# Spreading an expert search over the matrix work of a fused linear-attention and mixture-of-experts kernel

## The chip, the cores and the metric

The kernel runs on one core of a Trainium2 chip. The time is the device time of one execution in microseconds; three executions of the kernel before gave 408.66, 408.78 and 409.49, so the median is 408.78. A profile of one further execution shows where the time goes. Its engines are called PE (matrix products; PEld is the loading of their stationary operand), DVE (vector), ACT (scalar), POOL (GpSimd, which here also issues indirect DMAs) and SP (which issues the other DMAs).

## The reference

The first part is a linear-attention recurrence over 4 batches, 8 heads, 768 steps and a head size of 48. Its output, seen as 3072 rows (tokens) of 384 numbers, is the input of a mixture of 8 experts with a balanced assignment:

```python
logits = x @ w_gate                      # 3072 x 8
order = np.argsort(-logits.flatten())
for idx in order:                        # greedy, largest logit first
    tok, e = idx // E, idx % E
    if assigned[tok] >= 0 or counts[e] >= cap: continue     # cap = 384
    assigned[tok] = e; counts[e] += 1
for e in range(E):
    h = np.maximum(x[assigned == e] @ w1[e], 0.0)           # 384 -> 1024
    out[assigned == e] = h @ w2[e]                          # 1024 -> 384
```

Each expert gets exactly 384 tokens. The reference run on the given inputs fills the experts in the order 4, 3, 7, 5, 0, 6, 2, 1.

## The kernel before

**Two halves.** The class `Mild` computes the attention, in 24 units of 128 tokens, and writes the rows to memory. The class `Assignment` (called `walk`) finds the assignment without the sort: it repeatedly finds the next expert that fills up, with its 384 tokens. One such finding is called a search here. The class `Experts` multiplies: for each expert it gathers the 384 rows (`gather`, indirect DMAs on POOL), loads two weight matrices of 1.5 MB (`load_weights`, on SP), turns the rows (`turn`, L1509), computes the hidden layer (`hidden`, 24 products `h_ps`, L1518), and the second layer.

**A search** (`likely_steps`) is a generator that stops at each `yield`. It has three rounds. In a round DVE compares all tokens with 16 thresholds (`ind`), PE counts (`counts`, L925, three small products), DVE makes `own`, `cnt` and `wide`, PE adds over the partitions (`counts`, L936), and DVE narrows the thresholds (`most`, `full`, `dg`, `cand`, `low`). After the third round DVE makes `acc` and PE `st_ps` (L1056, L1057). `tokens` turns the found set into a list of row numbers: `row`, `oh`, `vals` on DVE, `some_ps` on PE (L1389), `part`, `list_ps` (L1407), `tok`. `book` checks what was found and `leave` takes its tokens out. Every round thus goes from DVE to PE and back twice.

**The early star.** Before all logits are known, one expert is chosen as the star (expert 1 with these inputs, the last to fill) and 256 of its tokens are computed early, by `early` of `Experts` (`e_xT_ps`, `e_h_ps`, `e_o_ps`), in pieces that `go(m)` interleaves with the searches for the first and second expert. Its last 128 tokens are computed at the end.

**Second layer.** Experts 1 to 5 in order of finding take two of their three token blocks by a scheme of seven products instead of eight (`seven`): sums of blocks of the hidden layer (S1 to S4, 128x512) and of the weights (T1 to T4, 128x768), made on DVE by `sums_of` (L1569), then seven groups of four products `p_ps` (L1591) and `SEVEN_OUT` sums (L1600). The third block is computed plainly by `result` (eight products `o_ps`, L1618). Experts 6 and 7 use a scheme of fifteen products. The tiles of the T sums have one buffer each, so expert n+1's T3 can be written only when PE has used expert n's.

**The order.** `run` loops over the experts. At its top it pulls the generator `later` until that yields a fetched expert; during the products it pulls twice more (`at_product`). Since the star can be among the experts found, `later` waits with a fetch: expert n is fetched only when the search after it is done, and `choose` takes the later one if the star has passed. `walk.ok` is cleared when a check fails, and at the end a branch on it (`If`) computes everything again in a general way. The attention, the early pieces and the first searches have an order written out by hand (`manual_schedule`); from `x.open_rest` on, a scheduler sets the order of each engine's instructions when the kernel is built.[...]

## Time and profile before

| what | value |
|---|---|
| median of three runs | 408.78 us |
| profiled execution | 408.76 us |
| its span in the profile | 406.9 us |
| PE busy | 383.4 us, 94% |
| DVE busy | 272.6 us, 67% |
| ACT, POOL busy | 160.6 us, 141.2 us |
| granted PE clock, mean | 0.992 |
| memory traffic | 139 GB/s over the span |

The span is from the first to the last event of the profile; 1.86 us of the execution lie outside it. The page cuts the span into 40 slices; the attention lies in the first thirteen or so, the experts after it. In the timeline view a line gives a start, a duration, engine, line of the program, operation and tiles, the number of records, and in brackets how long the engine had been idle and what ended it. A product of 32-bit numbers leaves two records.

### The profile page before, as it was taken

To read this page: it belongs to the slowest core of one execution; us is meant where nothing else is said; L and a number is where in the kernel's file an instruction comes from. 1 tells how busy PE (TensorE), PEld (TensorE's weight loads), DVE (VectorE), ACT (ScalarE), POOL (GpSimd) and SP (SyncE) were. 2 spreads that over 40 slices of the span, in tenths; PEclk is the share of its full clock that TensorE was granted. 3 is DMA by queue.
4 is the path that set the end of the run, shared out by engine and by line. 5 is a ranking of instruction groups with operands and counts; after the bars stand their busy time and mean duration, and the time that the engine had idled before them with its cause. 6 is when DMAs were issued, how large, how long until landed. Compare 5 with 4: busy or idle time off the path is not lost. (4 is left out here: it accounts for less than half of the span.)

```text
span 406.9 us, 8688 instructions
## 1 busy us (share of the span) xinstructions
PE 383.4 (94%) x3236; PEld 290.0 (71%) x3236; DVE 272.6 (67%) x948; ACT 160.6 (39%) x419; POOL 141.2 (35%) x173
## 2 busy tenths in 40 slices
PE   7789999999999887998999999999999999999993
PEld 5678888788877654568558657756856956966991
DVE  6675777576885788889387577578658852971630
ACT  4887878788872310221221221222212312132130
POOL 8787877666732021103303303202302222040020
PEclk9999999999999999999999999999999999999998
DMA  9999998887591282009218109108217365180010
GB/s 120 163 178 196 191 185 165 154 166 154 131 314 40 80 287 100 20 4 345 77 47 324 40 23 363 43 19 313 76 39 246 122 215 214 34 335 21 2 60 26
DMA packets 95331, 57.29 MB, mean 141 GB/s; under 512 B 77232, under 2 KB 89520, under 8 KB 95280
## 3 DMA queue, kind: packets, MB, share of 16 engines
q1 hardware_dynamic: 91520, 47.19, 46.4%
q0 software_dynamic: 3104, 9.44, 6.5%
q8 instruction: 27, 0.44, 0.5%
q14 instruction: 24, 0.20, 0.2%
q10 hardware_dynamic: 656, 0.01, 0.1%
HBM read 47.20 MB, written 9.44 MB: 139 GB/s over the span
## 5 line engine op out<-in xcount | busy, mean ns | idle before, releaser
L1518 PE MATMUL h_ps<-xT,w 128*128 128x384 f32 (+1 forms) x384 | 122.1, 469 | 0.6 <-ACT xT L1510 0.6
L1518 PEld LDWEIGHTS h_ps<-xT,w 128*128 128x128 f32 x384 | 65.6, 190 | 36.7 <-issue 3.6
L1520 ACT ACTIVATE hid<-h_ps 128x384 f32<-128x384 f32 (+1 forms) x64 | 29.7, 464 | 93.3 <-PE h_ps L1518 89.8
L1494 POOL DMA_INDIRECT xg<-x_rows,tok x22 | 22.9, 1039 | 112.3 <-issue 69.6
L494 ACT ACTIVATE AT<-ident,dd 128x128 f32<-128x128 f32 x192 | 58.8, 390 | 3.4 <-DVE dd L448 3.4
L1612 POOL DMA_INDIRECT out_dram<-o_all,to x16 | 19.9, 1247 | 75.8 <-DVE o_all L1600 73.7
L507 DVE COPY_PREDICATED AT<-mask,g_ps 128x512 f32<-128x512 uint8 x48 | 32.6, 733 | 12.5 <-PE g_ps L503 12.2
L1595 ACT COPY res<-p_ps 128x384 f32<-128x384 f32 (+2 forms) x28 | 13.2, 473 | 59.0 <-PE p_ps L1591 59.0
L1618 PE MATMUL o_ps<-w,hid 128*128 128x384 f32 x96 | 32.8, 486 | 0.0
L503 PE MATMUL g_ps<-rT,kT 48*128 48x128 f32 x384 | 28.6, 290 | 0.6 <-DVE AT L507 0.6
L436 POOL TENSOR_TENSOR kss<-krs,wk 128x384 f32<-128x384 f32 x24 | 24.3, 1014 | 9.3 <-DVE krs L340 8.1
L503 PEld LDWEIGHTS g_ps<-rT,kT 48*128 48x128 f32 x384 | 24.1, 193 | 3.8 <-PE rT_ps L458 1.1
L541 PE MATMUL y_ps<-AT,vts 128*64 128x128 f32 x384 | 25.7, 276 | 0.0
L443 POOL TENSOR_TENSOR rk<-rk,u_bc 128x384 f32<-128x384 f32 x24 | 24.2, 1007 | 1.9
L442 POOL TENSOR_TENSOR rk<-krs 128x384 f32<-128x384 f32 x24 | 24.5, 1021 | 0.2 <-DMA krs<-in_r_dram 0.2
L1618 PEld LDWEIGHTS o_ps<-w,hid 128*128 128x128 f32 x96 | 17.4, 190 | 9.8
L541 PEld LDWEIGHTS y_ps<-AT,vts 128*64 128x64 f32 x384 | 20.6, 137 | 1.0 <-issue 0.3
L1569 DVE TENSOR_TENSOR H<-hid 128x512 f32<-128x512 f32 x12 | 7.9, 687 | 19.1 <-ACT hid L1520 19.1
L1591 PE MATMUL p_ps<-T,S 128*128 128x192 f32 x120 | 20.7, 327 | 0.0
L559 ACT COPY x<-y_ps 128x512 f32<-128x512 f32 x24 | 14.0, 583 | 16.0 <-PE y_ps L541 16.0
L1591 PEld LDWEIGHTS p_ps<-T,S 128*128 128x128 f32 x120 | 19.6, 190 | 0.0
L477 DVE TENSOR_TENSOR rT<-rT_ps,WR 112x512 f32<-112x512 f32 x23 | 15.8, 685 | 4.4 <-PE rT_ps L458 4.4
(303 smaller groups left out, 687.4 us busy)
## 6 DMA issues: line engine op xcount, KB each, us to landing
w<-in_moe_w_dram SPq DMA_DIRECT2D x18, 1536.0 KB, 9.0
krs<-in_k_dram SPq DMA_DIRECT2D x24, 192.0 KB, 4.2
krs<-in_r_dram SPq DMA_DIRECT2D x24, 192.0 KB, 4.7
vts<-in_v_dram SPq DMA_DIRECT2D x24, 192.0 KB, 4.7
x_rows<-xr SPq DMA_DIRECT2D x24, 192.0 KB, 3.1
xg<-x_rows,tok POOLq DMA_INDIRECT x22, 4.4
out_dram<-o_all,to POOLq DMA_INDIRECT x16, 2.9
out_dram<-o_sb,to POOLq DMA_INDIRECT x5, 2.6
```

The source lines that it names most:

```text
L436: self.nc.gpsimd.tensor_mul(self.kss[:, n % self.NS].rearrange("p (g h) d -> p g h d", g=2)[:, :, :, 0:D], src, self.wk.rearrange("p (g h) ...
L442: nc.gpsimd.tensor_mul(rk, self.krs[:, n % self.NK, 1, 0:H, 0:D], self.krs[:, n % self.NK, 0, 0:H, 0:D])
L443: nc.gpsimd.tensor_mul(rk, rk, self.u_bc)
L494: nc.scalar.mul(AT[:, z, a, :], self.ident, dd[:, h:h + 1])
L503: nc.tensor.matmul(g_ps[:, z, a, :], kT[rows, a, :], rT[rows, a, :], start=True, stop=True)
L507: nc.vector.copy_predicated(out=AT[:, z], mask=self.mask.unsqueeze(1).to_broadcast([128, HP, T]), data=g_ps[:, z])
L541: nc.tensor.matmul(yv[q * PD:(q + 1) * PD, o // 2, o % 2, :], lhsT, rhs, start=(o // 2, q) not in seen, stop=stop, skip_group_check=True)
L1494: nc.gpsimd.indirect_dma_start(out=xg[:, c, :], out_offset=None, in_=x_dram[0:within, :], in_offset=bass.IndirectOffsetOnAxis(ap=tok[:, c: ...
L1518: nc.tensor.matmul(h_ps[:, 0:m], w1[:, f, ts(j, 128)], xT[:, f, 0:m], start=(f == 0), stop=(f == KD - 1))
L1520: nc.scalar.activation(hid[:, j, 0:m], h_ps[:, 0:m], AF.Relu)
L1591: nc.tensor.matmul(ps[:, q, :], left[a][:, j, :], right[b][:, j, :], start=(j == 0), stop=(j == KF // 2 - 1))
L1618: nc.tensor.matmul(o_ps, hid[:, j, ts(c, 128)], w2[:, j, :], start=(j == 0), stop=(j == KF - 1))
```

## The change

Experts two to four are fetched as soon as their own search is done, without the search that follows. For them `book(first=True)` is used, which clears `ok` if the found expert is the star: that case is left to the general part. From expert five on the former scheme holds. The search steps during experts 1, 2 and 3 are given out at 5, 7 and 9 points, counted in a progress from 0 to 2 (hidden layer 0 to 1, products 1 to 2), instead of two points in the products. The T sums of the first expert run come after its first sum of the hidden layer, and not before the hidden layer. The pieces of the star's second layer are grouped differently among the steps of the second search.

```diff
-        def hidden(self, w1, xT, m, half=lambda hid: None):
+        def hidden(self, w1, xT, m, half, progress):
...
                 if j == KF // 2 - 1:
                     half(hid)
+                progress((j + 1) / KF)
...
-                nc.vector.tensor_tensor(out=t, in0=at[a], in1=at[b], op=op)
+                last = nc.vector.tensor_tensor(out=t, in0=at[a], in1=at[b], op=op)
                 at[name] = t
+            return last
...
-        def run(self, ahead, later, rows):
-            xT = self.turn(ahead)
+        def run(self, ahead, later, rows, pulls={}):
+            xT, lead = self.turn(ahead), True
             while ahead:
...
-                right = (self.fifteen_w2 if many else self.seven_w2)(w2) if whole else None
+                late, lead = lead and not many, False
+                right = (self.fifteen_w2 if many else self.seven_w2)(w2) if whole and not late else None
                 left = {}
+                some = pulls.get(n, 2)
+                due = [1.55, 1.75] if some == 2 else [0.75 + 1.15 * i / (some - 1) for i in range(some)]
 
                 def half(hid):
+                    nonlocal right
                     for name, (i, j) in self.BLOCKS.items():
                         left[name] = hid[:, ts(j, KF // 2), ts(i, 128)]
-                    self.sums_of(left, self.EARLY_SUMS if many else self.SEVEN_EARLY)
+                    last = self.sums_of(left, self.EARLY_SUMS if many else self.SEVEN_EARLY)
+                    if late:
+                        with tc.issue_after(last.ins):
+                            right = self.seven_w2(w2)
+
+                def progress(t):
+                    nonlocal xT
+                    while due and t > due[0]:
+                        due.pop(0)
+                        next(later, None)
+                        if many and not due and ahead:
+                            xT = self.turn(ahead)
 
                 def at_product(part):
-                    nonlocal xT, stage
-                    if stage == 0 and part > 0.55 or stage == 1 and part > 0.75:
-                        next(later, None)
-                        stage += 1
-                        if many and stage == 2 and ahead:
-                            xT = self.turn(ahead)
+                    progress(1 + part)
...
-                go(6)
-                for m in (2, 3, 2, 3):
+                go(8)
+                for m in (2, 4, 2, 99):
                     next(search)
                     go(m)
-                go(99)
...
             walk.bound(ident)
-            was = second
+            now = second
+            for n in range(2, 5):
+                walk.book(now, first=True)
+                yield x.fetch(n, now["fmax"], walk.tokens(now["place"]))
+                walk.leave(now)
+                yield
+                now = walk.new_outs()
+                yield from walk.likely_steps(**now)
+            was = now
             walk.book(was)
             walk.leave(was)
-            for n in range(2, E):
+            for n in range(5, E):
...
-        x.run((1, xg, to, *have["v"]), later(), (a for a in [*out_rows[2:NT - 1], None]))
+        x.run((1, xg, to, *have["v"]), later(), (a for a in [*out_rows[2:NT - 1], None]),
+              {1: 5, 2: 7, 3: 9})
```

More of the change, by code (lines that the diff above doesn't have):

```diff
@@ L1522, in hidden @@
                     half(hid)
+                progress((j + 1) / KF)
             return hid
-        BLOCKS =        BLOCKS = dict(h0=(0, 0), h1=(0, 1), h2=(1, 0), h3=(1, 1), h4=(2, 0), h5=(2, 1))
+        BLOCKS = dict(h0=(0, 0), h1=(0, 1), h2=(1, 0), h3=(1, 1), h4=(2, 0), h5=(2, 1))
         SEVEN_EARLY = (("S3", "h0", SUB, "h2"),)
@@ L1634, in run @@
                 ahead = next((a for a in later if a), None)
-                right = (self.fifteen_w2 if many else self.seven_w2)(w2) if whole else None
+                late, lead = lead and not many, False
+                right = (self.fifteen_w2 if many else self.seven_w2)(w2) if whole and not late else None
                 left = {}
+                some = pulls.get(n, 2)
+                due = [1.55, 1.75] if some == 2 else [0.75 + 1.15 * i / (some - 1) for i in range(some)]
                 def half(hid):
+                    nonlocal right
                     for name, (i, j) in self.BLOCKS.items():
                         left[name] = hid[:, ts(j, KF // 2), ts(i, 128)]
-                    self.sums_of(left, self.EARLY_SUMS if many else self.SEVEN_EARLY)
-                def at_product(part):
-                    nonlocal xT, stage
-                    if stage == 0 and part > 0.55 or stage == 1 and part > 0.75:
-                        next(later, None)
-                        stage += 1
-                        if many and stage == 2 and ahead:
-                            xT = self.turn(ahead)
-                stage = 0
-                hid = self.hidden(w1, xT, nb * 128, half if whole else lambda hid: None)
+                    last = self.sums_of(left, self.EARLY_SUMS if many else self.SEVEN_EARLY)
[9 more added lines that the diff above has]
+                            xT = self.turn(ahead)
+                def at_product(part):
+                    progress(1 + part)
+                hid = self.hidden(w1, xT, nb * 128, half if whole else lambda hid: None, progress)
                 if whole:
```

## The prediction

> **What bounds the kernel now.** First the page, for the busiest engine:

> ```profile
> PE 383.4 (94%) x3236; PEld 290.0 (71%) x3236; DVE 272.6 (67%) x948; ACT 160.6 (39%) x419; POOL 141.2 (35%) x173
> ```

> PE sets the time, so only its gaps can be won. The chain that ended last covers only the last 15 us and does not help. Next, busy time by stretches, and PE's waits from 147 to 200 us:

> ```profile
> 150.00:170.00 20.00, 15.54 (x67) 8.63 (x66) 17.90 (x83) 3.21 (x7) 3.38 (x3) 1.00 0.30 114
> 190.00:200.00 10.00, 8.75 (x41) 5.72 (x41) 4.78 (x13) 2.30 (x6) 5.30 (x4) 1.00 0.43 160
> 200.00:210.00 10.00, 10.00 (x40) 5.56 (x39) 7.63 (x39) 2.33 (x5) 0.97 (x1) 1.00 0.06 22
> ```

> ```profile
> PE counts L925 <- DVE ind L913: 1.6, 1, 1.6
> PE counts L936 <- DVE wide L913: 1.5, 1, 1.5
> PE xT_ps L1509 <- DMA xg<-x_rows,tok: 1.1, 1, 1.1
> ```

> From 200 to 390 us the waits view names none. The gaps lie where the early star ends and expert 1 begins, and where expert 1 ends. The timeline of PE there (two records make one product):

> ```profile
> 147.30 3.39 PE L1685 MATMUL e_o_ps<-w,e_hid 128*128 128x384 f32 x10
> 152.31 0.26 PE L925 MATMUL counts<-prop,ind 128*128 128x64 bf16 x3 [1.62 <-DVE ind L913]
> ...
> 155.43 0.22 PE L936 MATMUL counts<-wide,ones_h 128*128 128x128 f16 x1 [1.49 <-DVE wide L913]
> ...
> 162.60 0.87 PE L1509 MATMUL xT_ps<-ident,xg 128*128 128x128 f32 x6 [0.48 <-ACT e_o_sb L1689]
> ...
> 164.87 1.56 PE L1518 MATMUL h_ps<-xT,w 128*128 128x384 f32 x4 [0.57 <-ACT xT L1510]
> ...
> 193.04 0.99 PE L1509 MATMUL xT_ps<-ident,xg 128*128 128x128 f32 x6 [1.11 <-DMA xg<-x_rows,tok]
> ...
> 199.69 0.22 PE L936 MATMUL counts<-wide,ones_h 128*128 128x128 f16 x1
> ```

> And DVE at the first two gaps: the four T sums of expert 1 stand between the steps of the second search.

> ```profile
> 150.49 0.95 DVE L1569 TENSOR_TENSOR T<-w 128x768 f32<-128x768 f32 x1
> 151.70 0.55 DVE L913 TENSOR_TENSOR ind<-m,cand 128x384 bf16<-128x384 f32 x1
> 152.17 0.95 DVE L1569 TENSOR_TENSOR T<-w 128x768 f32<-128x768 f32 x1
> 153.17 0.95 DVE L1569 TENSOR_TENSOR T<-w,T 128x768 f32<-128x768 f32 x1
> 154.22 0.95 DVE L1569 TENSOR_TENSOR T<-T,w 128x768 f32<-128x768 f32 x1
> 155.09 0.28 DVE L913 TENSOR_TENSOR wide<-digit_of,cnt 128x128 f16<-128x128 f32 x1
> ```

> [...] `wide` started at 155.09, behind a T it does not need, with `cnt` long ready (154.30). [...] So I count from start to start, which shows a little more than the brackets: the five products from 147.30, at 0.66, let the next instruction start near 150.6; it started at 152.31, so the gap is 1.7.

> **Prices, from start to start.** `h_ps`, `o_ps` 0.645 (seven `o_ps` from 227.59 to 232.11); `p_ps` 0.325 (eight from 216.69 to 219.29); xT of an expert 0.99; a `counts` set 0.09 and 0.08 more for the product behind it; the L936 product 0.06 and 0.05; `st_ps` 0.06, `some_ps` 0.15, `list_ps` 0.03. DVE: `wide` ready 1.2 after the set starts; the next `ind` 1.9 after the L936 product starts; `acc` 2.19 after it (163.31 to 165.50).

> **The change, part by part.** All PE, ACT, POOL and SP instructions stay, 4637 on PE in both builds; ACT, POOL and SP keep their order too. DVE loses nine short ones of about 0.1 us. What changes is the order on PE and DVE, from 147 us to the third block of expert 4; behind that the two builds have the same PE order. So I follow PE through the new order, and the difference at that point is the answer.

> *Star's end and turn.* Without the T's `ind` ends at 151.5; seven products now precede it and end at 151.9: no wait. `wide` 153.2 against PE at 153.3, next `ind` 155.3 against 156.0, next `wide` 157.3 against 157.5: no waits. But now only one `e_o_ps` stands behind the second L936 (four before). It is through at 158.24; ACT copies it, and xT, which takes its bank, starts at 158.98 (wait 0.74, as 161.86 to 162.60 before, where a `counts` set filled 0.09 of it). The third `ind` comes at 159.93, because seven short `book` instructions (158.78 to 159.85 before) are still in front of it (wait 0.28). The third part of the turn waits for ACT's first copy (160.13), `h_ps` for `wide` and ACT's last copy: 161.25 instead of 164.87. **Won: 3.62.**

> *Expert 1.* Hidden: 24 x 0.645 + searches 0.84 = 16.32, to 177.57 (before 181.93, with two more search rounds in it). The list of expert 2 is asked for at 167.6; `vals` ends at 167.5. The T sums follow S3 at about 171, 4 x 0.95 to 175, in DVE idle time before the products need T3 at 180.3; without that cover they cost 3.8. The second set is asked for 7.3 us into the products. In front of its `ind` DVE has T3 of expert 2, held until PE has used expert 1's (181.84 to 182.7), `most`, `full`, `dg` to 183.3, T1 to 184.2, and 0.9 more: 185.09, PE being there at 185.0. Products and third block: 28 x 0.325 + 0.99 + 8 x 0.645 + two sets 0.5 + a wait of 0.09 = 15.85, to 193.42 (before 199.69). The wait for xg is gone (about 1.35 by starts): its row numbers are ready near 170, not at 187.7, and POOL has nothing in front but two star scatters long done. On SP expert 2's weights are asked for near 163.5 instead of 181.7; their buffers are free since the star's second layer, the next weights in that queue are not known before 197, and the DMA engines moved 2 GB/s from 170 to 180 us.

> *Experts 2 to 4.* The fixed work is 15.48 + 9.10 + 0.99 + 5.16 = 30.73; before, with its search, each took 32.42 (199.69, 232.11, 264.53, 296.96). New: expert 2 has 4 sets, 4 L936, two `st_ps` and a list, 1.54, and waits of 0.17 (`st_ps`), 0.13 and 0.12 in the products: 32.7. There DVE has S1, S2, S4 (0.69 each) and the next expert's T3, T1, T2, each held until PE has read the old one, between the search's steps; I laid these out step by step. From the end of the hidden layer: `own` 0.3, `cnt`, S1 0.72 (when ACT is through), `wide` 1.64, S2, `most` 2.2, S4 to 3.1, `full` to `low` 3.65, an output sum, `ind` 4.6 against PE at 4.5; T3 to 5.5, `own`, T1 6.0 to 6.85 (when its product is through), `wide` 7.2 against PE at 7.07. Expert 3: 1.24 of searches, waits 0.18, 0.16 and 0.2, 0.3 of restarts: 32.7. Expert 4, with the ends of two searches: 1.41, and 0.2 before `st_ps`, 0.38 before `some_ps`: 32.8. Expert 4 ends at 291.65 instead of 296.96.

> Expert 5's rows become known in expert 4's products: `tok` 6.3 before xT needs them; for expert 2 before, `tok` (187.69) to xT (193.04) took 5.35. Cover 0.95. Its weights are asked for 19 us before its hidden layer; landing takes 6.7 to 11.4. Its T3 may be held for them on DVE (weights asked for at 14.0 of this expert, T3 due at 21.5), and behind it stands `own` of a set that PE issues at 25.2 and needs at the end of the expert only.

> **Sum.** 296.96 - 291.65 = 5.3 us. Own time 408.76 - 5.3 = 403.46; the median was 0.02 above the profiled execution, so **403.5**.

> **Unshown.** No operation is new, but S sums, T sums and search steps never shared DVE in products before. Upper bound: each of the five sets so placed one T late (0.95), 4.8 in all; lower bound: none of the nine waits that I give for experts 1 to 4, 1.6 less. I take my layout, since each of its durations is in the trace.

> **Rivals.**
> 1. Half a T late in each of the five sets: 2.4 lost, **405.9**. For it: DVE was 11.46 of 11.5 us busy from 180.5 to 192 with one set there. Against: DVE idled 5.2 and 4.4 us in the third blocks of experts 1 and 2, where a part of the work now goes.
> 2. Expert 5's rows late, as expert 2's were: up to 1.35, **404.8**. Against: the cover above.
> 3. Slower, by one mechanism: DVE's queue in the products of experts 1 to 3. A set held behind two T's costs 1.9; five cost 9.5, **413.0**. It decides from 1.2 us a set. Against: each T waits only for products that end 1.3 us apart, and 0.95 fits between.
> 4. The change does not do its work: expert two to four is the star, `ok` falls and all is computed again, about twice the time. The fill order 4, 3, 7, 5 and star 1 exclude it, unless the chosen star differs; the second fewest of the counts that choose it are 230 and 232, the latter expert 6, also late.
> 5. Nothing moves (the gaps close into new ones of the same size): 408.8. Against: new waits of 5 us would be needed and I find 2.

> **Chances.** Mine 0.79, own range 402.2 to 404.6; rival 1 0.10, 2 0.04, 3 0.04, 4 0.01, 5 0.02. Runs differ by some 0.2%, and less than that counts as no change. The range 402.2 to 406.0 takes in mine, 1 and 2. Faster 0.93, same 0.02, slower 0.05.

> **What would show it.** T sums right behind S3; no DVE-caused wait above 0.4 between 150 and 158; no wait for xg at the end of expert 1; `h_ps` of expert 1 near 161.3; the start of expert 5's hidden layer near 291.7. Wrong if waits on `ind` or `wide` in the products pass 0.5, or a T stands before `own` for over 1 us.

## The result, and the profile after

The changed kernel takes **404.36 us** (median of 403.25, 403.27, 405.45 and 406.39), the kernel before 408.72 beside it; the ratio is 0.9895, 95% interval 0.9846 to 0.9944. The two lower values and the two higher ones are 2 to 3 us apart. The profile is of the highest, and what sets it apart lies in the first 35 us of the kernel, which the change doesn't touch; it is taken up last.

PE's busy time is 2.4 us longer than before, which comes from half the clock in those first 35 us (0.50 from 25.14 to 31.97; in e8, a second profile of the changed kernel, it is 383.4, as before). Its waits between 147 and 300 us are nearly gone. From the page of the changed kernel, from its busy time by stretches (columns: stretch, its length, then PE, PEld, DVE, ACT and POOL with their instructions, PE clock, DMA share, GB/s), and from its waits of PE (total us, times, longest):

```profile
PE 385.8 (95%) x3236; PEld 293.0 (72%) x3236; DVE 269.6 (67%) x939; ACT 161.0 (40%) x419; POOL 138.4 (34%) x173
```

```profile
150.00:170.00 20.00, 19.02 (x76) 11.14 (x77) 16.76 (x91) 3.66 (x8) 4.83 (x5) 1.00 0.56 195
190.00:200.00 10.00, 10.00 (x44) 6.23 (x43) 6.29 (x27) 2.63 (x6) 3.03 (x3) 1.00 0.16 59
200.00:210.00 10.00, 10.00 (x39) 5.81 (x38) 7.28 (x41) 2.46 (x5) 1.95 (x2) 1.00 0.77 267
```

```profile
PE xT_ps L1509 <- ACT e_o_sb L1700: 0.6, 1, 0.6
PE counts L936 <- DVE wide L913: 0.4, 1, 0.4
```

From 150 to 170 us PE is busy for 19.0 instead of 15.5. The waits of 1.6 for `ind`, 1.5 for `wide` and 1.1 for `xg` are gone. PE's timeline from the star's second layer on, and behind it two lines of the kernel before:

```profile
150.53 4.68 PE L1696 MATMUL e_o_ps<-w,e_hid 128*128 128x384 f32 x14
155.04 0.25 PE L925 MATMUL counts<-prop,ind 128*128 128x64 bf16 x3
...
162.14 0.88 PE L1509 MATMUL xT_ps<-ident,xg 128*128 128x128 f32 x6 [0.57 <-ACT e_o_sb L1700]
...
164.23 0.22 PE L936 MATMUL counts<-wide,ones_h 128*128 128x128 f16 x1 [0.39 <-DVE wide L913]
...
172.21 0.17 PE L1407 MATMUL list_ps<-part,alike 128*128 128x12 f16 x1
...
190.41 0.82 PE L1509 MATMUL xT_ps<-ident,xg 128*128 128x128 f32 x6
...
294.69 2.15 PE L1518 MATMUL h_ps<-xT,w 128*128 128x384 f32 x6
```

```profile
186.94 0.17 PE L1407 MATMUL list_ps<-part,alike 128*128 128x12 f16 x1
...
297.01 2.15 PE L1518 MATMUL h_ps<-xT,w 128*128 128x384 f32 x6
```

The first `e_o_ps` stands at 150.53, and at 147.30 before, though PE's order in front of it is the same. So all distances below are counted from the first `e_o_ps`: to expert 1's first `h_ps` (the "star's end"), to the `list_ps` of expert 2 (the "list"), and to expert 5's first `h_ps` (the "stretch"). The stretch was 297.01 - 147.30 = 149.71 and is 294.69 - 150.53 = **144.16**: 5.55 shorter. It repeats well: four profiles with this order of PE gave 144.16, 143.87, 143.88 and 144.01 (the changed kernel, e8, e9, e12), two with the order before 149.71 and 149.69 (e11), so that differences of under 0.3 say nothing. On DVE the T sums now stand behind S3, in time that DVE has to spare (it idles 3.3 us after them):

```profile
173.69 0.69 DVE L1570 TENSOR_TENSOR S<-hid 128x512 f32<-128x512 f32 x1 [0.28 <-ACT hid L1520]
174.30 1.82 DVE L1570 TENSOR_TENSOR T<-w 128x768 f32<-128x768 f32 x2
176.16 0.96 DVE L1570 TENSOR_TENSOR T<-w,T 128x768 f32<-128x768 f32 x1
177.15 0.96 DVE L1570 TENSOR_TENSOR T<-T,w 128x768 f32<-128x768 f32 x1
181.43 0.69 DVE L1570 TENSOR_TENSOR S<-hid 128x512 f32<-128x512 f32 x1 [3.33 <-ACT hid L1520]
```

### The profile page after: what moved, and what is told of

The parts are those of the page before. It is cut to its first block, busy times and chain, and to the rows that moved or that the text cites. A ratio compares the mean times of both kernels' runs of the same rounds, so it can differ in the third digit from the quotient of the medians.

```text
span 404.6 us, 8676 instructions
## 1 busy us (share of the span) xinstructions
PE 385.8 (95%) x3236; PEld 293.0 (72%) x3236; DVE 269.6 (67%) x939; ACT 161.0 (40%) x419; POOL 138.4 (34%) x173
## 5 line engine op out<-in xcount | busy, mean ns | idle before, releaser
L1518 PE MATMUL h_ps<-xT,w 128*128 128x384 f32 (+1 forms) x384 | 120.1, 466 | 0.0
L1518 PEld LDWEIGHTS h_ps<-xT,w 128*128 128x128 f32 x384 | 66.7, 190 | 38.6 <-issue 1.8
L1614 POOL DMA_INDIRECT out_dram<-o_all,to x16 | 17.7, 1105 | 102.0 <-DVE o_all L1602 69.5
L541 PE MATMUL y_ps<-AT,vts 128*64 128x128 f32 x384 | 26.6, 282 | 0.0
```

The costliest lines, as they stand in the source:

```text
L541: nc.tensor.matmul(yv[q * PD:(q + 1) * PD, o // 2, o % 2, :], lhsT, rhs, start=(o // 2, q) not in seen, stop=stop, skip_group_check=True)
L1518: nc.tensor.matmul(h_ps[:, 0:m], w1[:, f, ts(j, 128)], xT[:, f, 0:m], start=(f == 0), stop=(f == KD - 1))
```

## The experiments

All distances, in us from the first `e_o_ps`. Each of e1 to e7 was run once.

| kernel | expert 1's h_ps | list, expert 2 | expert 2's h_ps | expert 5's h_ps |
|---|---|---|---|---|
| before | 17.57 | 39.64 | 52.45 | 149.71 |
| changed | 13.89 | 21.68 | 46.12 | 144.16 |
| e1: T sums later, alone | 14.95 | 39.54 | 50.93 | 148.19 |
| e2: pieces regrouped, alone | 16.06 | 39.42 | 52.36 | 149.61 |
| e5: both of these | 13.89 | 40.19 | 53.32 | 150.59 |
| e3: new fetching, alone | 17.58 | 24.73 | 49.36 | 153.73 |
| e4: changed, not spread | 13.89 | 21.69 | 45.66 | 149.94 |
| e6: new fetching and spreading | 17.58 | 24.74 | 49.82 | 147.62 |
| e7: changed, `ind` three times | 13.89 | 21.69 | 46.18 | 148.46 |

### One part at a time

e1 keeps only the late T sums, e2 only the new grouping `go(m)`, e3 only the new `later`. The edits are against the changed kernel. In e1 and e2 `later` is the old one as well (not shown), and in e1 to e4 nothing is spread:

```diff
 # e1 and e3: pieces as before
-                go(8)
-                for m in (2, 4, 2, 99):
+                go(6)
+                for m in (2, 3, 2, 3):
...
+                go(99)
 # e2 and e3: T sums early
-                late, lead = lead and not many, False
+                late, lead = False, False
 # e1 to e4: two pulls for each expert
-        x.run((1, xg, to, *have["v"]), later(), (a for a in [*out_rows[2:NT - 1], None]),
-              {1: 5, 2: 7, 3: 9})
+        x.run((1, xg, to, *have["v"]), later(), (a for a in [*out_rows[2:NT - 1], None]))
```

> The kernel before with one part of the change: expert 1's T sums come after its first sum of the hidden layer. The measure is the stretch from the first e_o_ps (147.30 before) to expert 5's first L936 product, 149.66 us before and 144.10 after. By the prediction's accounting the four T's in DVE's queue are what ends the waits of 1.62 and 1.49 us. Without them ind is ready at about 151.5, but with the old grouping only five e_o_ps (through at 150.6) stand in front of it, so 0.9 of the first wait stays and the second goes: about 2.2 to 2.6 won, stretch 147.2, time 406.3. If the grouping of the pieces was the main thing and the T's only filled time, less than 1 is won (stretch above 148.7). The wait for xg at the end of expert 1 (1.1 by the bracket) stays.

Measured: 409.04 us beside 409.15; 1.5 us of the gain is hidden by low clock in the first 35 us, behind which the first `e_o_ps` stands at 148.77. The star's end won 2.62, as expected from its one wait of 0.9 that stayed. But expert 2's list came at 39.54, where it had come before (39.64), and at the end of expert 1 PE waits longer for the rows. The whole stretch won 1.52, not 2.2 to 2.6. The waits of PE and the list in e1:

```profile
PE xT_ps L1509 <- DMA xg<-x_rows,tok: 1.9, 2, 1.4
PE counts L925 <- DVE ind L913: 0.9, 1, 0.9
```

```profile
188.31 0.17 PE L1407 MATMUL list_ps<-part,alike 128*128 128x12 f16 x1
```

> The kernel before with only the new grouping of the star's pieces. With the T's still in DVE's queue, ind comes at 152.3 against seven pieces through at 151.9: a wait of 0.4 in place of 1.62, so 1.2 of PE work moved in front; but the wait for wide (1.49) stays and the later rounds have fewer pieces to cover them, so that some of it comes back: 0.3 to 1.3 won, stretch 148.4 to 149.4. If the grouping is the main thing, 2.5 or more. The wait for xg stays.

Measured: 408.84 beside 409.15. Won at the star's end 1.51; list at 39.42; the waits for the rows rose from 1.1 to 2.6 in all (the first line below), and of the 1.51 only 0.10 is left at expert 5, less than was expected at the least. So neither part is "the main thing": of what PE wins ahead of the list it waits for a part behind it, 1.1 of 2.6 in e1 and nearly all in e2. The list stays where it is, and DVE, which prepares it, has hardly any time to spare: from the first `e_o_ps` to the list its idle stretches of over 0.25 us, nearly all ended by a count from PE, sum to 4.0 us of 39.6 before, 3.4 in e1 and 3.6 in e2.

```profile
PE xT_ps L1509 <- DMA xg<-x_rows,tok: 2.6, 3, 1.6
PE counts L936 <- DVE wide L913: 1.9, 2, 1.5
```

> The kernel before with only the new rule of fetching (experts two to four as found), with two pulls in the products as before. By the accounting the wait for xg at the end of expert 1 goes (1.35 by starts) and nothing is won at the star's end: stretch about 148.3, time 407.4. If the search steps, now unspread, gather in one place and wait there for DVE, the gain is eaten and the stretch is 149.7 or more.

Measured: **416.41**, 7.3 slower than before, the opposite of the first expectation; 1.7 of it is low clock in the first 35 us, and the stretch is 4.0 longer. Expert 2's rows are in time (its first `h_ps` comes at 49.36 instead of 52.45, which is 3.1 earlier and more than the 1.35 of the wait, since a part of the search work now comes later), but from expert 4's first `h_ps` to expert 5's it is 39.99, against 32.42 before, with a wait of 3.7 for expert 5's rows:

```profile
PE xT_ps L1509 <- DMA xg<-x_rows,tok: 3.9, 2, 3.7
```

> The changed kernel without the spreading: two pulls in each expert's products instead of 5, 7 and 9 points. If spreading carries part of the gain, searches now gather at the end of the products and at the start of the next expert, and DVE's waits return there: stretch above 145.1 (over 1 us longer than the 144.10 of the changed kernel). If the gain is all from T's, grouping and fetching, as the prediction's sum has it (3.62 at the star's end, 1.35 at xg, the rest small), stretch 144.1 to 144.6.

Measured: 415.07. Leaving out the spreading costs 149.94 - 144.16 = **5.8** up to expert 5. It is lost at one place (7.0 between expert 4's first `h_ps` and expert 5's; ahead of that e4 is 1.2 earlier), and not by DVE's waits in the products but by the rows of expert 5. From expert 5 on a fetch needs the search after it too, so two searches have to be done in expert 4's time. With two pulls the first of them is still under way in expert 4's hidden layer (its `st_ps` at 269.74) and the second ends late in the products (284.90). PE's waits of e4, and where expert 5's search ends in it (the changed kernel has this `some_ps` at 278.95, before any product of expert 4's third block):

```profile
PE xT_ps L1509 <- DMA xg<-x_rows,tok: 4.3, 2, 3.7
```

```profile
287.31 2.10 PE L1620 MATMUL o_ps<-w,hid 128*128 128x384 f32 x6
289.46 0.31 PE L1389 MATMUL some_ps<-vals,row 128*128 128x48 f16 x6
...
297.38 0.55 PE L1509 MATMUL xT_ps<-ident,xg 128*128 128x128 f32 x3 [3.70 <-DMA xg<-x_rows,tok]
```

The wait has a second part. Behind it PE's clock was at half for 6.8 us, of which this line shows six:

```profile
299.00:305.00 6.00, 5.43 (x15) 3.00 (x14) 0.80 (x3) 0.96 (x2) 1.67 (x2) 0.50 0.25 94
```

PE being busy for 6.3 us of the 6.8, half of that is lost by estimate (at a clock of 0.50 an `o_ps` of e5 takes 1.28 from start to start, from 198.15 to 199.43, where 0.645 stood at full clock): 3.1, of which 2.4 lie behind expert 5's first `h_ps` (from there to the end of the span it is 413.3 - 300.50 = 112.8, and 110.4 in e8). In all the spreading is worth about 8 here, by estimate 5 by the late rows and 3 by the clock.

### Do the parts add up?

e5 has both parts at the star's end and the old fetching; e6 the rest of the change, with T sums and pieces as before. (The spreading with the old fetching was not run.)

```diff
 # e5
-            now = second
-            for n in range(2, 5):
...
-            was = now
+            was = second
...
-            for n in range(5, E):
+            for n in range(2, E):
...
-        x.run((1, xg, to, *have["v"]), later(), (a for a in [*out_rows[2:NT - 1], None]),
-              {1: 5, 2: 7, 3: 9})
+        x.run((1, xg, to, *have["v"]), later(), (a for a in [*out_rows[2:NT - 1], None]))
 # e6
-                late, lead = lead and not many, False
+                late, lead = False, False
...
-                go(8)
-                for m in (2, 4, 2, 99):
+                go(6)
+                for m in (2, 3, 2, 3):
...
+                go(99)
```

> The kernel before with both parts at the star's end (T sums later, pieces regrouped), but with the old fetching and two pulls. Measure: from the first e_o_ps to the first h_ps of expert 5, 149.71 us before and 144.16 after. Additive (the prediction's sum): the star's end gives its 3.6 and the wait for xg keeps the 1.35 it had, so about 146.1. Chain (from the two runs with one part each): the list of row numbers for expert 2 came 39.5 us after the first e_o_ps in both and in the kernel before (39.4 to 39.6), so it is set by DVE's chain of two searches and not by PE; what PE wins before it, it waits for at xg: list at 39.4 to 39.9, waits for xg of 2.5 to 4, stretch 148.2 to 149.6.

Measured: the stretch is 150.59, **0.9 longer than before**, though the star's end won its full 3.68. The list comes at 40.19, later than in any other kernel, and DVE's timeline shows why: the T sums, late as in e1, stand in the middle of the second round of the next search, the first (at 174.71) just ahead of `most`, the other three between `most` and `cand`:

```profile
175.57 0.28 DVE L1024 TENSOR_REDUCE most<-counts 128x16 f32<-128x128 f32 x1
175.78 0.94 DVE L1570 TENSOR_TENSOR T<-w 128x768 f32<-128x768 f32 x1
176.64 0.16 DVE L1026 TENSOR_SCALAR full<-most 128x16 f32<-128x16 f32 x1
176.75 0.96 DVE L1570 TENSOR_TENSOR T<-w,T 128x768 f32<-128x768 f32 x1
177.63 0.16 DVE L1028 TENSOR_REDUCE dg<-full 128x1 f32<-128x16 f32 x1
177.75 0.96 DVE L1570 TENSOR_TENSOR T<-T,w 128x768 f32<-128x768 f32 x1
178.62 0.23 DVE L1030 SCALAR_TENSOR_TENSOR cand<-cell,dg,base 128x16 f32<-128x16 f32 x1
```

```profile
PE xT_ps L1509 <- DMA xg<-x_rows,tok: 3.1, 1, 3.1
```

From expert 1's first `h_ps` to the list it is 26.30 in e5 and 22.07 before: 4.2 more, about the four T's of 0.95 that went there. They eat the 3.68 of the star's end and 0.55 more. (In e1 three of them stand in this chain too, ahead of its third `ind`.) PE then waits 3.1 for the rows, and behind that wait its clock is at half here too:

```profile
190.00:196.00 6.00, 4.38 (x21) 2.68 (x19) 5.96 (x25) 0.80 (x2) 3.05 (x3) 1.00 1.05 407
197.00:203.00 6.00, 5.54 (x15) 3.87 (x16) 0.95 (x1) 1.44 (x3) 1.95 (x2) 0.50 0.30 103
```

That is about 2.9 of the stretch (5.8 us of work at half). Without it some 147.7 would stand, by this estimate, and both expectations fall: against 146.1 for parts that add up, 1.6 of the 3.6 went into the longer wait, and against 148.2 or more for a chain that gives everything back, some was kept. What the list took away and what the clock took away make a loss together. (The run's 413.38 us hold 3.4 more of low clock, from the first 35 us.)

> The changed kernel with the T sums and the grouping of the kernel before, that is with the new fetching and the spreading alone. Additive and chain theory agree on the star's end (nothing won there, 17.6 us to the first h_ps of expert 1) and on the xg wait (gone). If the parts add up: stretch 144.16 + 3.6 = 147.8, from 31.8 to 32.2 for expert 1. If early fetching and spreading carry nearly all, and the star's parts are only made good by them, below 146.

Measured: 406.92, stretch 147.62; the first expectation (147.8) held. The first two waits of before are all there again:

```profile
PE counts L925 <- DVE ind L913: 1.6, 1, 1.6
PE counts L936 <- DVE wide L913: 1.5, 1, 1.5
```

So the new fetching with its spreading wins 2.1 alone; the parts at the star's end would win 2.0 alone on a full clock, and lost 0.9 in the run, but win 147.62 - 144.16 = 3.5 once the rows of expert 2 no longer come at the end of that chain.

### What a late search step costs

```diff
+    times = 1
...
-        tt(ind, self.by_token(m, ND), self.by_expert(cand), ALU.is_ge)
+        for _ in range(self.times):
+            tt(ind, self.by_token(m, ND), self.by_expert(cand), ALU.is_ge)
...
+                walk.times = 3
                 yield from walk.likely_steps(**now)
+                walk.times = 1
```

> The changed kernel with every comparison with the thresholds (ind) in the searches for experts three to five made three times over, so that each of these nine rounds comes some 0.95 us later (two more of 0.5) on DVE. This prices the prediction's third rival, a search step that is late behind DVE's queue. If each step is as tight as the prediction laid out (PE arrives within 0.1 to 0.2 us of ind in the products), PE waits up to 0.95 in each of the nine: 4 to 8 us, time 407.5 to 411.5 on an undisturbed clock, with waits for ind in the list. If there is slack in most places, under 2 us. The stretch from the first e_o_ps to the first h_ps of expert 5 (144.16) tells it without the clock.

Measured: 410.88, 3.0 of it low clock in the first 35 us; the stretch is 148.46, 4.3 longer. The size is at the lower end of the first expectation, the place is another: hardly any wait for `ind` or `wide`. The scheduler shifts the late rounds in PE's order behind more products: in expert 4's time one `counts` set stands some seven products later. Two of the three searches make it good before their list is due: those of experts 3 and 4 come 0.1 and 1.0 late. The third doesn't, and it is paid by `xT` of expert 5, whose list comes at 283.43 - 150.32 = 133.11, against 129.95 in the changed kernel: a wait of 2.2, and 1.7 for 3.4 us at half clock behind it. Its waits of PE:

```profile
PE xT_ps L1511 <- DMA xg<-x_rows,tok: 2.2, 1, 2.2
...
PE counts L938 <- DVE wide L914: 0.5, 2, 0.4
```

### The first 35 us

The difference of 3.23 ahead of the first `e_o_ps` lies in the granted PE clock. Busy time from 25 to 30 us in the kernel before, and then in the changed one (last columns: PE clock, DMA share, GB/s):

```profile
25.00:30.00 5.00, 5.00 (x79) 4.31 (x80) 3.81 (x9) 4.79 (x14) 4.36 (x5) 1.00 1.04 204
```

```profile
25.00:30.00 5.00, 5.00 (x52) 4.40 (x50) 2.00 (x6) 2.97 (x10) 2.88 (x3) 0.51 1.36 195
```

PE has been idle just ahead of it in both, for 1.57 and 1.67 us. e9 and e11 fill that idle stretch with products that nobody reads, in the changed kernel and in the one before; e8 is the changed kernel once more; e10 and e12 have the filling and one more edit at the star's end.

```diff
 # e9, e10, e11 and e12
+                if n == 2:
+                    self.idle(6, "g_ps")
                 if 1 < n <= N - B:
                     self.rows((n - 1,), "few")
 # e10 and e12
-                o_ps = ps.tile([128, DX], F32, name="e_o_ps", tag=("y_ps", "g_ps")[c % 2])
+                o_ps = ps.tile([128, DX], F32, name="e_o_ps", tag=("g_ps", "y_ps")[c % 2])
 # e10
-                go(8)
-                for m in (2, 4, 2, 99):
+                go(7)
+                for m in (2, 3, 2, 99):
```

> The changed kernel once more, unedited. Its own profile had half the PE clock from 25.4 to 31 us, and the work from there on stood 3.2 us later. By the accounting the change is worth 5.5 on an undisturbed clock: about 403.3 where that stretch is undisturbed, up to 406.5 where it is not, so the executions should fall into a lower cluster near 403.3 and a tail above; the median lies anywhere between 403.3 and 405.5. If instead the change itself costs time there, all executions lie above 405.

> The changed kernel with six unread products of ident with itself on PE ahead of the x_ps at 24.5 us, which fill the idle 1.6 us that precedes the half clock in the profiles. If the idle stretch is what sets the clock back, the clock is 1.00 from 24 to 35 us in every profile, the executions lie within 0.3 of each other, and the median is 403.3 (1 to 2 below the unedited one's, if that has disturbed executions in its median). If the idle stretch is not the cause, the same spread up to 406 stays, and 0 to 1 us is lost to the added products.

> The kernel before with the same filled gap, to have both kernels on the same clock: 408.7 if it runs undisturbed as its median does, so that the change is worth 5.3 to 5.6 between the two filled kernels, by the stretch that does not depend on the clock at 25 us (149.71 against 144.16). If the filling itself costs, both are later by the same amount.

| kernel | executions, us | median |
|---|---|---|
| before | 27: sixteen from 408.97 to 409.31, eleven from 409.76 to 412.65 | 409.12 |
| before, gap filled (e11) | 22: all from 408.86 to 409.42 | 409.04 |
| changed (e8) | 403.06, 403.15, 403.22, 403.40, 404.78, 405.41 | 403.31 |
| changed, gap filled (e9) | 403.02, 403.14, 403.24, 403.29, 403.32 | 403.24 |

The tail is in the unfilled kernels, before and changed alike, and gone in the filled ones (the highest of e12 below, 403.76, is 0.5 above its median). So the idle stretch is the cause, in the sense that filling it removes the effect (the clock is 1.00 from 24 to 35 us in the profiles of e9 to e12). The filling takes away the tail and nothing else (e9 is at 0.9841 of before, interval 0.9805 to 0.9877; its lowest executions are no lower than the unedited one's). Between the two filled kernels the change is worth 409.04 - 403.24 = **5.80**, and the stretches 149.69 (e11) and 143.88 (e9) give 5.81. Of the idle 1.6 us there remain, in e9:

```profile
23.19 0.85 PE L418 MATMUL unread_ps<-ident 128*128 128x128 f32 x6 [0.42 <-DVE AT L507]
24.36 0.60 PE L590 MATMUL x_ps<-ident,x 112*128 112x112 f32 x4 [0.33 <-ACT x L559]
```

> The same with two edits at the star's end: the two banks of e_o_ps are exchanged, so that the turn of expert 1 takes the bank that was freed first, and one piece fewer stands in front of the second search (7, then 2, 3, 2, the rest). The wait of 0.6 of xT for the copy of e_o should go; if it is then ind or wide that PE waits for, nothing is won. 0.3 to 0.6 won over the kernel with the filled gap, 402.8; stretch from the first e_o_ps to expert 5's first h_ps, less what moved in front of it, 143.6.

Measured: 403.59, 0.35 more than e9; the expectation missed. The wait for the copy of `e_o` fell from 0.57 to 0.22, but waits for ACT's copies of `xT`, 0.20 and 0.57, and 0.23 for `ind` took its place; expert 1's first `h_ps` comes at 14.31 instead of 13.89.

> The kernel with the filled gap, with the two banks of e_o_ps exchanged and nothing else (PE's order stays the same). It tells why the last edit at the star's end won nothing. If the wait of 0.57 of xT for the bank is on the path that sets the end, it goes and 0.4 to 0.6 is won: 402.7. If DVE's chain of the second search sets the end of the turn (ind ends at 159.48, wide at 160.70 in the kernel with the filled gap, and neither depends on that bank), the wait moves to ind and wide: 403.2, the first h_ps of expert 1 still 13.9 us after the first e_o_ps.

Measured: 403.30, expert 1's first `h_ps` at 13.89: nothing won, as the second expectation had it, but not for its reason. The wait did not move to `ind` and `wide`, it stayed where it was:

```profile
PE xT_ps L1511 <- ACT e_o_sb L1702: 0.6, 1, 0.6
PE counts L938 <- DVE wide L915: 0.4, 1, 0.4
```

So the exchange of the banks doesn't take that wait away, and e10's loss is then from the regrouping. What else ties this `xT` to the copy was not tried. Little hangs on it: in e9 `ind` ends at 159.48 and the set that reads it starts at 159.53, so that without the wait the set, and `wide` and `h_ps` behind it, could come 0.05 earlier by this estimate.

## Why the prediction was right, point by point

Forecast 403.5, measured 404.36, inside the range; on an undisturbed clock about 403.3.

**Star's end.** Forecast won 3.62, measured 17.57 - 13.89 = 3.68. Less the 3.23 by which the profile stands later, `h_ps` is at 161.19; 161.25 was forecast. Of the waits given for it, `xT` has 0.57 by the bracket (0.74 by starts was forecast) and `wide` 0.39; none is shown for the third `ind`.

**Expert 1.** 34.82 to 32.17 was forecast, a gain of 2.65; measured 34.88 to 32.23, 2.65. The wait for `xg` is gone, and the T sums are hidden.

**Experts 2 to 4.** Forecast 98.23 for the three, measured 98.04 in this profile and 97.74 in e8, where 97.26 stood before. The waits given for the products are not in PE's view; in that of PEld, L925 waits for `ind` six times between 177 and 300 us, 1.4 in all and 0.3 at most. What comes back is 0.5 to 0.8, not 1.0. (The terms given for experts 3 and 4 add up to 32.81 and 32.72, where 32.7 and 32.8 stand; the total is the same.)

**Expert 5's rows.** `tok` was to come 6.3 before `xT` and came 6.6 before it. Too small was the 5.35 for the way from `tok` to `xT`, read from a single wait for expert 2's rows: where PE waited for expert 5's, it was 6.1 (e3, e4) and 6.5 (e7). So there was next to no cover, not 0.95: in the profile of the changed kernel the first part of `xT` runs 1.05 instead of 0.82, so about 0.2 was waited there; in e8 nothing was. That the rows were in time was in part luck.

**Sum.** Forecast 5.3; measured 5.55 here and 5.81 between the filled kernels. The time is 0.9 above the forecast because of the two high ones of the four executions: one had the low clock in its profile, and the other (405.45), of which there is no profile, lies where e8 has its tail. The prediction took everything in front of 147 us as equal. It is, but only on the same clock (the first `e_o_ps` at 147.05 in e9 and at 147.15 in e11).

**Where the working was weaker than its number.** The sum lists 3.62 for the star's end and 1.35 for `xg` as gains of their own. They are not: with the old fetching the rows of expert 2 came at the end of a chain on DVE (list at 39.4 to 40.2 us in all four kernels), and a part of what PE won ahead of it was waited for behind it: 1.1 of 2.6 in e1, 1.4 of 1.5 in e2, 1.7 of 3.7 in e5, without the clock. The number held because PE was followed through the full new order, in which the row numbers are "ready near 170" (`tok` at 172.65 - 3.23 = 169.4). The sentence that without their cover the T sums cost 3.8 named the right price: e5 shows 4.2. And the spreading was never priced; it is worth 5.8 up to expert 5 (e4), more with what the clock takes behind it.

**Rivals.** The second named the tight place, expert 5's rows. In the changed kernel it cost 0.2 at most, but "up to 1.35" would not have bounded it: where the search ended 3.2 us later PE waited 2.2 (e7), and without the spreading 3.7 (e4). The third named the right resource and the wrong place: lateness on DVE isn't paid by each set (e7 has 0.5 of such waits in all), it is handed on to the next gather. The first, a half T lost in each set, didn't show as a loss: `own` does come 0.6 to 0.9 late behind a T in three sets, but no wait for `ind` is in PE's view. The fourth and fifth did not come about.

**What would show it.** All five signs are there: T sums behind S3, no wait from DVE above 0.4 in the stretch named, none for `xg`, `h_ps` at 161.19, expert 5's hidden layer at 294.69 - 3.23 = 291.46 for 291.7. Neither sign of being wrong is: PE has no wait in the products, and a T kept `own` back for 0.9 at most.

## What to carry to other kernels

Before adding up gaps on the busiest engine, ask which chain on another engine ends at the next wait behind them: here, while the row numbers came at a fixed time, a gap closed ahead of them moved behind them in good part, and waits of 2.2 to 3.7 us cost 1.7 to 3.1 more for the clock. A chain that hops between engines is worth following to its end: in e7 its lateness was not shown where it arose but at the one transfer that depended on it, and giving out its steps early and evenly was worth 5.8 us here. And compare two profiles from a common landmark behind which they differ, not from the start of the execution.

## What the runs showed of the hardware

Where the grid lies against the gap doesn't settle it. In the six the half clock began 0.4 to 2.0 us after the end of the gap. But in the kernel before a point of its grid, by estimate at 25.32 (8.25 and five units of 3.413), came 0.8 after the end too, and the clock stayed at 1.00. So something else has a part in it, which these runs don't show.
